# Keys of pairs 13 and 14 loaded whole instead of in parts of three quarters and one quarter

## The chip, the cores and the metric

The kernel runs on one core of one Trainium2 chip. The metric is the device time of one execution in microseconds (us), as a median of several runs.

## The reference

One token of width 512 is normalised; it then goes through attention over a cache of 8192 keys and values for each of 32 heads, and through a small gated block whose result gates the attention's output:

```python
# x [1,1,512], k_cache and v_cache [1,32,8192,128], wq [512,4096], wo [4096,512], all float32
xn = layernorm(x)
q = (xn @ wq) as 32 heads of 128
p = softmax(q . k_cache * 128 ** -0.5)          # per head, over 8192 keys
s = (p . v_cache, heads joined) @ wo
g = silu((sigmoid(xn @ w_gate) * (xn @ w_up)) @ w_down)
out = x + s * g
```

Keys and values are 268 MB; nothing in them is used twice.

## The kernel before

Heads are worked off in 16 pairs (0 to 15). A pair's keys, like its values, fill one buffer: 128 partitions (64 for each head) with 128 positions of 128 numbers each, which is 64 KB a partition and 8 MB in all. There are three such buffers, named slots: keys alternate between two of them (pair i in slot (i+1) % 2), all values go through the third. After the last pair, the output weights wo (8 MB) go into the slot that held pair 14's keys.

All loads of keys, values and wo are issued by SyncE (SP) on one queue, in the order of the code, each behind its waits. `load_keys(i, ...)` waits until pair i-2's scores have been summed, that is until its slot is free; `load_values` waits until PE is done with the values before. From pair 2 on the order is: keys of pair i, then values of pair i-1. Values of pairs 14 and 15 are loaded in halves and smaller parts (`V_CUTS`), the first half as soon as PE has used the first half of the values before.

For each pair, VectorE (DVE) multiplies the keys by the query in place (line 415), sums each product over 128 numbers (line 416), and takes the maximum of the scores (line 418). `K_CUTS` tells for which pairs the keys come in parts; for each part DVE waits for its load, multiplies and sums. Then PE turns the maxima so that DVE can reduce them to one for each head (`all_max`, line 408), ScalarE (ACT) computes the exponentials, which are the weights (`powers_of`, line 430), and PE weighs the values with them in a burst of 64 matmuls (`pair`, tile `slot,zeros`). ACT copies the result out, PE picks the diagonal blocks out of it (tile `o,pick`), and DVE turns them (`heads_out`, line 423).

After pair 15 the heads are divided by the softmax sums and turned into a column (line 472). Then comes the product with wo, loaded in nine pieces (`W_ENDS`): DVE takes 17 of the 32 row blocks (`W_DVE`, lines 513 and 515) and adds its two partial sums (line 518), PE takes 11 others; DVE adds the two results (`to_fold`, line 490), PE folds that into the accumulator that already holds rows 28 to 30 (`fold`), adds the last row, 31, and DVE gates and adds x (lines 537, 539). PE's instructions are all recorded under line 38; its groups are told apart by their tiles.

Of the kernel before, what the change touches and what calls it, by code (L numbers as in the profile page):

```python
# [51 lines left out]
def kernel(  # L52
# [18 lines left out]
    NB = S // HP  # L71
    NP = H // 2
# [18 lines left out]
    W_ENDS, W_FOLD = (10, 16, 20, 23, 26, 28, 30, 31, 32), 28  # L91
    W_PE = [0, 1, 10, 16, 17, 20, 21, *range(24, W_FOLD)]
    W_DVE = [r for r in range(W_FOLD) if r not in W_PE]
    V_CUTS, K_CUTS = (NB // 2, NB * 13 // 16), {NP - 3: (NB * 3 // 4,), NP - 2: (NB * 3 // 4,), NP - 1: (NB // 2,)}

    N_SEMS = 40
    DVE, ACT, SP, POOL = nc.vector, nc.scalar, nc.sync, nc.gpsimd
    PE = Later(nc.tensor)
    pe_only = OrderedEngineSet([nc.tensor.engine])
# [2 lines left out]

    sems = [nc.alloc_semaphore(f"s_{i}") for i in range(N_SEMS)]
    s_out = nc.alloc_semaphore("s_out")
# [494 lines left out]
```

## Time and profile before

| | |
|---|---|
| median of 3 runs | 684.52 us (684.47 to 685.29) |
| the profiled execution | 684.89 us, span 683.4 us |
| busy share of the span: DVE, PE, ACT | 90%, 32%, 7% |
| loads | 293.67 MB, mean 430 GB/s |
| granted TensorE clock, mean | 0.668 of full speed |

Times in the timelines are microseconds from the span's start. A line gives the start, the duration, the engine, the line of the kernel, the operation, output and inputs by the program's names with their shapes, and how many instructions were merged; in brackets the idle time of the engine ahead of it and what ended it. SPq is SyncE's queue; its rows show when loads are issued, not when they land. PEq is PE's sequencer, which waits for semaphores.

### The profile page before, as it was taken

To read this page: it belongs to the slowest core of one execution; us is meant where nothing else is said; L and a number is where in the kernel's file an instruction comes from. 1 tells how busy PE (TensorE), PEld (TensorE's weight loads), DVE (VectorE), ACT (ScalarE), POOL (GpSimd) and SP (SyncE) were. 2 spreads that over 40 slices of the span, in tenths; PEclk is the share of its full clock that TensorE was granted. 3 is DMA by queue.
4 is the path that set the end of the run, shared out by engine and by line. 5 is a ranking of instruction groups with operands and counts; after the bars stand their busy time and mean duration, and the time that the engine had idled before them with its cause. 6 is when DMAs were issued, how large, how long until landed. Compare 5 with 4: busy or idle time off the path is not lost. (4 is left out here: it accounts for less than half of the span.)

```text
span 683.4 us, 3400 instructions
## 1 busy us (share of the span) xinstructions
PE 216.2 (32%) x1376; PEld 62.0 (9%) x1376; DVE 615.2 (90%) x156; ACT 44.6 (7%) x142; POOL 2.6 (0%) x11
## 2 busy tenths in 40 slices
PE   0353024060513206050412406050422406060666
PEld 0120001010100101010100101010100101010110
DVE  3879999999999998998989899898989999999917
ACT  2130010000000101000000100000010101000010
POOL 0000000000000000000000000000000000000000
PEclk9996657575665757575665757575665757575886
DMA  9999999999999999999999999999999999999998
GB/s 382 429 440 472 430 430 430 430 430 430 430 430 430 430 430 430 430 456 456 437 430 430 430 430 430 430 430 430 430 430 445 449 441 399 476 399 430 430 430 337
DMA packets 7552, 293.67 MB, mean 430 GB/s; under 512 B 856, under 2 KB 864, under 8 KB 1664
## 3 DMA queue, kind: packets, MB, share of 16 engines
q1 hardware_dynamic: 7544, 293.67, 99.5%
q10 hardware_dynamic: 8, 0.00, 0.0%
HBM read 293.67 MB, written 0.00 MB: 430 GB/s over the span
## 5 line engine op out<-in xcount | busy, mean ns | idle before, releaser
L415 DVE TENSOR_TENSOR slot<-slot,q_all 128x16384 f32<-128x16384 f32 (+3 forms) x19 | 275.9, 14522 | 21.4 <-DMA slot<-in_A_k_cache_dram 21.4
L416 DVE TENSOR_REDUCE sc<-slot 128x128 f32<-128x16384 f32 (+3 forms) x19 | 276.0, 14525 | 0.7
L38 PE MATMUL psum<-slot,zeros 128*8 128x512 f32 x1024 | 145.5, 727 | 261.5 <-PEq L38 261.5
L38 PEld LDWEIGHTS psum<-slot,zeros 128*8 128x8 f32 x1024 | 30.2, 102 | 363.3 <-issue 363.3
L38 PE MATMUL psum<-ident,mx 128*1 128x128 f32 x32 | 8.7, 372 | 108.6 <-PEq L38 108.6
L437 ACT COPY o<-psum 128x512 f32<-128x512 f32 x16 | 9.4, 586 | 405.1 <-PE psum L38 405.1
L38 PE MATMUL psum<-slot,ones 128*128 (+3 forms) x36 | 15.9, 612 | 21.9 <-PEq L38 16.2
L290 DVE SCALAR_TENSOR_TENSOR slot<-slot,xn 128x1376 f32<-128x1376 f32 (+1 forms) x8 | 18.9, 2360 | 3.0 <-DMA slot<-in_A_wq_dram 2.7
L38 PE MATMUL psum<-o,pick 128*2 128x128 f32 x128 | 16.5, 272 | 12.8 <-PEq L38 12.8
L423 DVE STREAM_TRANSPOSE psum<-psum 32x128 f32<-32x128 f32 x16 | 5.0, 310 | 11.1 <-PE psum L38 11.1
L430 ACT ACTIVATE zeros<-sc,nb 64x128 f32<-64x128 f32 x32 | 12.8, 399 | 0.9
L38 PEld LDWEIGHTS psum<-o,pick 128*2 128x2 f32 x128 | 9.9, 84 | 29.6 <-issue 27.2
L428 ACT ACTIVATE nb<-psum 128x2 f32<-128x2 f32 x16 | 2.8, 172 | 150.9 <-PE psum L38 150.9
L38 PE MATMUL psum<-slot,o_all 128*1 128x128 f32 (+1 forms) x54 | 10.7, 510 | 5.3 <-DMA slot<-in_A_wo_dram 5.3
L38 PEld LDWEIGHTS psum<-ident,mx 128*1 128x1 f32 x32 | 1.9, 80 | 112.6 <-issue 112.6
L408 DVE TENSOR_REDUCE mx<-psum 1x2 f32<-1x128 f32 x16 | 4.4, 277 | 7.8 <-PE psum L38 7.8
L38 PE MATMUL psum<-zeros,rs 128*32 128x2 f32 x32 | 3.8, 188 | 23.5 <-PEq L38 23.5
L38 PE MATMUL psum<-mx,ones 1*128 1x2 f32 x32 | 8.4, 330 | 7.4 <-PEq L38 7.4
L515 DVE SCALAR_TENSOR_TENSOR q_all<-slot,o_all,q_all 128x512 f32<-128x512 f32 x15 | 10.0, 747 | 0.0
L38 PE MATMUL psum<-slot,o 128*1 128x512 f32 x26 | 5.5, 910 | 12.8 <-DMA slot<-in_B_w_down_dram 12.8
L38 PEld LDWEIGHTS psum<-slot,ones 128*128 128x128 f32 (+1 forms) x36 | 6.4, 201 | 31.3 <-issue 23.3
L38 PEld LDWEIGHTS psum<-mx,ones 1*128 1x128 f32 x32 | 7.5, 290 | 14.3 <-issue 14.3
(54 smaller groups left out, 60.5 us busy)
## 6 DMA issues: line engine op xcount, KB each, us to landing
slot<-in_A_k_cache_dram SPq DMA_DIRECT2D x2, 6144.0 KB, 37.9
slot<-in_A_v_cache_dram SPq DMA_DIRECT2D x3, 4096.0 KB, 22.7
slot<-in_A_wq_dram SPq DMA_DIRECT2D x2, 4096.0 KB, 16.3
slot<-in_A_k_cache_dram SPq DMA_DIRECT2D x2, 4096.0 KB, 40.5
slot<-in_A_k_cache_dram SPq DMA_DIRECT2D x2, 2048.0 KB, 42.4
slot<-in_B_w_gate_dram SPq DMA_DIRECT2D x1, 2752.0 KB, 26.7
slot<-in_B_w_up_dram SPq DMA_DIRECT2D x1, 2752.0 KB, 32.7
slot<-in_B_w_down_dram SPq DMA_DIRECT2D x1, 2560.0 KB, 24.1
```

The source lines that it names most:

```text
L38: ins = getattr(self.engine, name)(*args, **kwargs)
L290: return dve(DVE.scalar_tensor_tensor(y, w[:, k, cols], xn[:, k:k + 1], y, op0=ALU.mult, op1=ALU.add))
L408: DVE.reduce_max(mx[:1, 1:3], pt[0:1, :].rearrange("o (e p) -> o e p", e=2), axis=AX.X).then_inc(reduced, 1)
L415: wait(DVE, dve(DVE.tensor_mul(k[:, j, :], k[:, j, :], qb[:, i:i + 1, :].to_broadcast([P, n, Dh]))))
L416: summed[i] = dve(DVE.reduce_sum(sc[i % 2][:, j], k[:, j, :], axis=AX.X))
L423: turned_out[i] = dve(DVE.transpose(o, pn.rearrange("e (a r) -> e a r", r=WR)))
L428: wait(ACT, act(ACT.mul(nb, pm[:, :2], -SCALE)))
L430: ACT.activation(weights[h, :, e * HT:(e + 1) * HT], sc[i % 2][h].rearrange("p (g b) -> p g b", b=HT), AF.Exp, bias=nb[h, e:e + 1], scale= ...
L437: ACT.copy(o1, po).then_inc(copied, 1)
L515: ins = DVE.scalar_tensor_tensor(part[n], wo_t[:, r, :], col, part[n], op0=ALU.mult, op1=ALU.add)
```

## The change

Pairs 13 and 14 are taken out of the table of cuts, so their keys are loaded, multiplied and summed whole, as those of pairs 0 to 12 are. Pair 15 keeps its two halves. Two semaphores are no longer needed.

```diff
-    V_CUTS, K_CUTS = (NB // 2, NB * 13 // 16), {NP - 3: (NB * 3 // 4,), NP - 2: (NB * 3 // 4,), NP - 1: (NB // 2,)}
+    V_CUTS, K_CUTS = (NB // 2, NB * 13 // 16), {NP - 1: (NB // 2,)}
 
-    N_SEMS = 40
+    N_SEMS = 38
```

On DVE, at pair 14 (`slot` the keys, `q_all` the queries, `sc` the scores, `mx` the maxima):

```order
 L408 TENSOR_REDUCE mx<-psum 1x2
-L415 TENSOR_TENSOR slot<-slot,q_all 128x12288
-L416 TENSOR_REDUCE sc<-slot 128x96
-L415 TENSOR_TENSOR slot<-slot,q_all 128x4096
-L416 TENSOR_REDUCE sc<-slot 128x32
+L415 TENSOR_TENSOR slot<-slot,q_all 128x16384
+L416 TENSOR_REDUCE sc<-slot 128x128
 L418 TENSOR_REDUCE mx<-sc 128x1
 L423 STREAM_TRANSPOSE psum<-psum 32x4x32
```

Product and sum of three quarters and of one quarter become one product and one sum over all 128 positions; what stands ahead of them and behind keeps its place. Pair 13 changes in the same way.

On SP's queue, from the values of pair 12 on:

```order
 L227 DMA slot<-in_A_v_cache_dram 128x16384
-L168 DMA slot<-in_A_k_cache_dram 128x12288
-L168 DMA slot<-in_A_k_cache_dram 128x4096
+L168 DMA slot<-in_A_k_cache_dram 128x16384
 L227 DMA slot<-in_A_v_cache_dram 128x16384
 L168 DMA slot<-in_A_k_cache_dram 128x8192 x2
```

The two loads of pair 14's keys become one between the values of pairs 12 and 13; pair 15's keys still follow as two halves.

## The prediction

> **What bounds the kernel now.** I read the slices and the queue table of the page first, then the chain of waits, then the timelines of VectorE (DVE), TensorE (PE) and SyncE's queue (SP) over the last 220 us, last the granted clock. From the page:
>
> ```profile
> DMA  9999999999999999999999999999999999999998
> q1 hardware_dynamic: 7544, 293.67, 99.5%
> ```
>
> The one load queue keeps the 16 DMA engines busy for 99.5% of the span. Less compute cannot shorten that; only a dry queue, or a tail behind the last bytes that gets longer, can move the time. The chain that ended last:
>
> ```profile
> 641.64 5.35 PE psum L38 x32
> ...
> 650.71 28.58 DMA slot<-in_A_wo_dram
> ...
> 679.95 0.62 PE psum L38 x16
> ...
> 680.59 0.44 PE psum L38 x8
> ```
>
> It ends in the loads of wo, whose last pieces release the last products at 679.95 and 680.59. So DVE and PE may be late only by what they wait for wo. DVE's timeline (start, duration; in brackets the idle time before and who ended it):
>
> ```profile
> 467.47 17.23 DVE L415 TENSOR_TENSOR slot<-slot,q_all 128x16384 f32<-128x16384 f32 x1 [2.77 <-DMA slot<-in_A_k_cache_dram]
> ...
> 506.12 17.23 DVE L415 TENSOR_TENSOR slot<-slot,q_all 128x16384 f32<-128x16384 f32 x1 [2.80 <-DMA slot<-in_A_k_cache_dram]
> ...
> 540.64 0.29 DVE L418 TENSOR_REDUCE mx<-sc 128x1 f32<-128x128 f32 x1
> ...
> 541.90 12.94 DVE L415 TENSOR_TENSOR slot<-slot,q_all 128x12288 f32<-128x12288 f32 x1
> ...
> 576.65 0.29 DVE L418 TENSOR_REDUCE mx<-sc 128x1 f32<-128x128 f32 x1
> ...
> 578.62 12.96 DVE L415 TENSOR_TENSOR slot<-slot,q_all 128x12288 f32<-128x12288 f32 x1 [0.84 <-DMA slot<-in_A_k_cache_dram]
> ...
> 613.38 0.29 DVE L418 TENSOR_REDUCE mx<-sc 128x1 f32<-128x128 f32 x1
> ...
> 614.80 8.67 DVE L415 TENSOR_TENSOR slot<-slot,q_all 128x8192 f32<-128x8192 f32 x1
> ...
> 649.55 0.29 DVE L418 TENSOR_REDUCE mx<-sc 128x1 f32<-128x128 f32 x1
> ...
> 664.76 0.32 DVE L423 STREAM_TRANSPOSE psum<-psum 32x128 f32<-32x128 f32 x1 [10.40 <-PE psum L38]
> ...
> 665.34 0.21 DVE L472 STREAM_TRANSPOSE o_all<-psum 32x32 f32<-32x32 f32 x1
> 667.00 0.88 DVE L513 TENSOR_SCALAR q_all<-slot,o_all 128x512 f32<-128x512 f32 x2 [1.46 <-DMA slot<-in_A_wo_dram]
> 667.80 10.02 DVE L515 SCALAR_TENSOR_TENSOR q_all<-slot,o_all,q_all 128x512 f32<-128x512 f32 x15
> 677.86 0.69 DVE L518 TENSOR_TENSOR q_all<-q_all 128x512 f32<-128x512 f32 x1
> 679.15 0.69 DVE L490 TENSOR_TENSOR q_all<-q_all,psum 128x512 f32<-128x512 f32 x1 [0.60 <-PE psum L38]
> ```
>
> Pairs 11 and 12 (whole keys) wait 2.8 us for their keys; pairs 13 to 15 (in parts) hardly wait: DVE is ahead of the loads there. PE's timeline, from pair 3 on:
>
> ```profile
> 216.36 8.31 PE L38 MATMUL psum<-slot,zeros 128*8 128x512 f32 x64 [15.15 <-PEq L38]
> ...
> 525.55 9.02 PE L38 MATMUL psum<-slot,zeros 128*8 128x512 f32 x64 [19.91 <-PEq L38]
> ...
> 544.07 0.24 PE L38 MATMUL psum<-zeros,rs 128*32 128x2 f32 x2 [1.39 <-PEq L38]
> 564.24 8.45 PE L38 MATMUL psum<-slot,zeros 128*8 128x512 f32 x64 [19.93 <-PEq L38]
> ...
> 602.92 9.59 PE L38 MATMUL psum<-slot,zeros 128*8 128x512 f32 x64 [22.81 <-PEq L38]
> ...
> 631.94 5.30 PE L38 MATMUL psum<-slot,zeros 128*8 128x512 f32 x32 [14.99 <-PEq L38]
> ...
> 652.56 0.24 PE L38 MATMUL psum<-zeros,rs 128*32 128x2 f32 x2 [1.39 <-PEq L38]
> 652.71 7.72 PE L38 MATMUL psum<-slot,zeros 128*8 128x512 f32 x52
> 661.03 1.89 PE L38 MATMUL psum<-slot,zeros 128*8 128x512 f32 x12 [0.59 <-PEq L38]
> ...
> 680.17 0.40 PE L38 MATMUL psum<-q_all,ones 128*1 128x128 f32 x8
> ```
>
> A burst of 64 matmuls weighs one pair's values. Pairs 0 to 13 do it in one go, in 8.31 (pair 3, the shortest) to 9.59 us (pair 13, the longest of 14). Pair 15's burst, from 652.71, pauses at 52 for its last 1.5 MB and goes on at 661.03: what bounded it was the load, not PE.
>
> **The change, part by part.** It removes two loads and four instructions of DVE; the same bytes are loaded in the same order, and PE, ACT and POOL keep their instructions.
>
> *The loads.* Values of pairs 11, 12 and 13 arrived (first matmul of the burst) at 525.55, 564.24 and 602.92: 38.69 and 38.68 us apart, with the keys of 13 and 14 in two parts between them. Whole keys of pairs 11 and 12 arrived 38.65 us apart (467.47, 506.12). So a part more costs the queue 0.03 to 0.04 us; two fewer give at most -0.1 us. I count 0.
>
> *Arrival.* Whole keys of pair 13 arrive at 506.12+38.65 = 544.77, those of pair 14 at 583.42. DVE loses its early start: 541.90 becomes 544.77, 578.62 becomes 583.42.
>
> *DVE.* A whole pair takes 540.64-506.12 = 34.52 us to its maximum, one in two parts 576.65-541.90 = 34.75, so each merge gives 0.23 back. Pair 13 ends at 544.77+34.52 = 579.29 (+2.64), still before pair 14's keys; so pair 13's lateness goes no further on DVE. Pair 14 ends at 583.42+34.52 = 617.94 (+4.56). To the next product took 541.90-540.64 = 1.26 us; pair 15 starts at 619.20 instead of 614.80, its keys long there, and after 34.75 us (649.55-614.80) its maximum stands at 653.95: **+4.40 us**.
>
> *SP.* Its queue waits for exactly these ends:
>
> ```profile
> 572.76 0.33 SPq L227 DMA_DIRECT2D slot<-in_A_v_cache_dram  x1
> 576.64 0.81 SPq L168 DMA_DIRECT2D slot<-in_A_k_cache_dram  x2
> 609.14 38.68 SPq L227 DMA_DIRECT2D slot<-in_A_v_cache_dram  x5
> ```
>
> Pair 15's keys are issued at 579.3 instead of 576.64. The queue then holds the values of pair 13 (issued 572.76, landed 602.92): 23.6 us of cover, cost 0; without that cover 2.64 us. Behind it on SP stand pair 14's values, which wait for PE until 609.14 anyway. The issue of wo waits for pair 14's sums (617.94), but in SP's order it comes after pair 15's values at 647. Also 0.
>
> *PE before the tail.* Pair 13's weights are ready some 4 us after 579.29, values at 602.92; pair 14's at about 621.5, values at 631.94. Both covered, by 19 and 10 us.
>
> *Pair 15's values: the step that counts.* From maximum to the first matmul of the burst took 652.71-649.55 = 3.16 us; in pair 12, where PE had been idle longer, 544.07-540.64 = 3.43 to the matmul ahead of it, with 0.15 more 3.58. So the burst starts at 657.1 to 657.5, say 657.3, and its values are there by about 661: now it runs in one go, bounded by PE. How long depends on the clock:
>
> ```profile
> 604.00:608.00 4.00, 4.00 (x21) 0.67 (x17) 4.00 (x2) 0.00 (x0) 0.00 (x0) 0.50 0.91 393
> 608.00:612.00 4.00, 4.00 (x44) 1.00 (x36) 3.97 (x2) 0.00 (x0) 0.00 (x0) 0.99 1.12 483
> ...
> 652.00:656.00 4.00, 3.44 (x22) 0.83 (x26) 1.21 (x5) 0.57 (x3) 0.00 (x0) 0.57 1.05 451
> ```
>
> (PE's count is in the second column, the granted clock third from the end.) Pair 13's burst ran at 0.50 for the first 5 us, pair 15's got full clock only near 656. Of the 8.31 to 9.59 us I take the middle, 8.95: end at 666.25 instead of 661.03+1.89 = 662.92, **+3.33 us** (2.5 to 4.2 with both ends of start and burst).
>
> The Trainium skill, "TensorE: Matmul & The Clock Gate", Part 1, says that the clock is doubled after a busy window of some 3.4 us, and that windows run freely. Taken literally (a burst fills one whole window first, so it runs 3.4 to 6.8 us at half clock), and with pair 13's row as the measure (9.59 us with about 5 at half clock, each of which costs half a microsecond), an estimate is 8.7 to 10.4 us, an end at 666.0 to 667.7 and +0.7 to +2.4 us at the finish, +1.6 in the middle, where the rows give +1.0. The trace bears out the lower part of that alone: the longest of 14 bursts took 9.59, the shortest 8.31.
>
> *The tail's slack.* Behind the burst come a copy, picking matmuls and the transposes up to 665.55, which move with it. Then DVE waited for wo until 667.00: 1.4 us absorbed. Its 17 products (10.9 us) run back to back, so no other piece of wo was late for them. Its sum ended at 678.55, and the next addition waited for PE until 679.15: 0.6 absorbed. (PE's own rows of wo absorb the delay too, since they wait for pieces.) That addition ended at 679.84 and PE's folding began at 680.17: 0.3 absorbed. The last row waited for its piece until 680.59, within the folding's 0.40: 0 to 0.2. Together 2.35 (2.3 to 2.5).
>
> *Sum.* 3.33 - 2.35 = **+1.0 us** (ends 0 and +1.9). The profiled execution took 684.89 us (span 683.4 and 1.5 around it), so 685.9; it lies 0.37 above the median of the runs, 684.52, from which the sum is 685.5. I take the latter, since runs are compared by their median.
>
> **The rivals.** *Hidden altogether:* a short burst (8.31) from 657.1 ends at 665.4, +2.5, which the slack swallows: 684.5 to 684.9. For it: every wait of the tail is on wo. Against: the middle burst is a full microsecond over the slack.
>
> *The late clock (slower):* the mechanism is PE's clock in pair 15's burst. If it starts as unluckily as pair 13's (9.59 us from 657.3), it ends at 666.9, +4.0, at the finish +1.6: 686.1 from the median, 686.5 from the profiled run. It decides from a burst of 9.3 us on (3.7-2.35 = 1.37 us, which is 0.2%). For it: bursts cluster near 8.4, 8.95 and 9.5 from pair to pair, so which comes is chance.
>
> *A dry queue (slower):* if pair 15's keys had been what the engines waited for, the 2.64 us would all show: 687.2. It would need 23.6 us of lateness.
>
> *Fewer transfers pay (faster):* the queue is the bound, so a fixed price of each load would come straight off; from the rows 0.04 us each, at most 684.4, and only if the tail hides too. The Trainium skill, "DMA: Bandwidth & Descriptors", Anatomy of one DMA, gives about 2.0 us fixed for each (measured on another issue path than SP's), which by estimate would be 4 us less, 680.5; the arrivals 38.65 and 38.68 apart contradict that as a price of throughput.
>
> **How the numbers follow.** Something like 0.2% (1.37 us) is what a measurement of this kernel can tell. My forecast (+0.4 to +1.37) gets 0.42, hidden 0.20, the late clock or a tail worse than counted 0.30, the dry queue 0.03, faster 0.05. So faster 0.05, same 0.62, slower 0.33. The range goes from the hidden case (684.4) to the late clock from the profiled run (686.6).
>
> **What would show it.** Right: DVE's product of pair 14 starts near 583.4 after some 4 us of waiting for keys; its maximum of pair 15 stands near 654; the burst of pair 15 is one group of 64 ending at 665.4 to 667; DVE's first product with wo starts without a wait for wo near 668.5; folding waits for DVE, and the chain of waits ends over DVE and PE instead of the loads of wo; the DMA share stays above 99%. Wrong: if the keys of pair 14 come earlier than 582, if the values of pair 15 come later than 657, or if the load queue shows a gap near 579 or 603.

## The result and the profile after

The changed kernel takes 686.49 us (median of 19 runs, 685.18 to 688.49), before 685.0 us (19 runs, 684.47 to 685.43): +1.5 us, a ratio of 1.0022 with a 95% interval of 1.0015 to 1.0028. That is a hair beyond what was called "the same". The runs of the changed kernel also lie three times as far apart as those of before; a part of that is time outside the span, 2.3 and 2.5 us in the two longest runs against 1.5 in most, and the spans themselves lie between 683.7 and 686.0. The profiled execution took 685.76 us, its span 684.2 us; the median span of the 19 runs is 684.9, so this profile shows one of the luckier executions.

The load queue is as full as before, on the page of the changed kernel:

```profile
DMA  9999999999999999999999999999999999999997
q1 hardware_dynamic: 7256, 293.67, 99.3%
```

The same bytes come in 288 packets fewer. What differs is the chain that ended last. It no longer holds a load; it goes through DVE:

```profile
666.88 1.05 PE psum L38 x8
...
669.72 3.37 DVE q_all L515 x6
...
679.69 0.70 DVE q_all L518
...
680.49 0.70 DVE q_all L490
...
681.23 0.66 PE psum L38 x16
```

DVE's timeline of the changed kernel (columns as before) shows where the lateness comes from:

```profile
544.49 17.23 DVE L415 TENSOR_TENSOR slot<-slot,q_all 128x16384 f32<-128x16384 f32 x1 [2.97 <-DMA slot<-in_A_k_cache_dram]
...
583.16 17.23 DVE L415 TENSOR_TENSOR slot<-slot,q_all 128x16384 f32<-128x16384 f32 x1 [2.83 <-DMA slot<-in_A_k_cache_dram]
...
618.94 8.67 DVE L415 TENSOR_TENSOR slot<-slot,q_all 128x8192 f32<-128x8192 f32 x1
...
653.68 0.29 DVE L418 TENSOR_REDUCE mx<-sc 128x1 f32<-128x128 f32 x1
...
668.84 0.88 DVE L513 TENSOR_SCALAR q_all<-slot,o_all 128x512 f32<-128x512 f32 x2
```

Pairs 13 and 14 now wait for their keys as pairs 11 and 12 did. Pair 15's product starts at 618.94 instead of 614.80, its maximum stands at 653.68 instead of 649.55, and the first product with wo starts without a wait for wo. PE's timeline of the same kernel:

```profile
657.25 8.83 PE L38 MATMUL psum<-slot,zeros 128*8 128x512 f32 x64
...
681.23 0.40 PE L38 MATMUL psum<-q_all,ones 128*1 128x128 f32 x8 [0.72 <-DVE q_all L490]
```

Pair 15's burst is one piece now and ends at 666.08, 3.16 us later than before (662.92). The folding waits for DVE.

### The profile page after: what moved, and what is told of

It reads as the page before. It is cut to its first block, busy times and chain, and to the rows that moved or that the text cites. A ratio compares the mean times of both kernels' runs of the same rounds, so it can differ in the third digit from the quotient of the medians.

```text
span 684.2 us, 3394 instructions
## 1 busy us (share of the span) xinstructions
PE 221.2 (32%) x1376; PEld 62.5 (9%) x1376; DVE 615.3 (90%) x152; ACT 44.5 (7%) x142; POOL 2.6 (0%) x11
## 5 line engine op out<-in xcount | busy, mean ns | idle before, releaser
L415 DVE TENSOR_TENSOR slot<-slot,q_all 128x16384 f32<-128x16384 f32 (+1 forms) x17 | 275.6, 16213 | 27.7 <-DMA slot<-in_A_k_cache_dram 27.7
L416 DVE TENSOR_REDUCE sc<-slot 128x128 f32<-128x16384 f32 (+1 forms) x17 | 275.7, 16216 | 0.6
L38 PE MATMUL psum<-slot,zeros 128*8 128x512 f32 x1024 | 150.9, 755 | 256.4 <-PEq L38 256.4
```

Source lines behind the costliest of these rows:

```text
L38: ins = getattr(self.engine, name)(*args, **kwargs)
L415: wait(DVE, dve(DVE.tensor_mul(k[:, j, :], k[:, j, :], qb[:, i:i + 1, :].to_broadcast([P, n, Dh]))))
L416: summed[i] = dve(DVE.reduce_sum(sc[i % 2][:, j], k[:, j, :], axis=AX.X))
```

## The experiments

The theory in one line, as it stood after the two traces. DVE's gating (line 537) in the changed kernel, then in before:

```profile
681.92 0.29 DVE L537 TENSOR_TENSOR g_row<-g_row,psum 128x128 f32<-128x128 f32 x1 [0.74 <-PE psum L38]
```

```profile
681.05 0.29 DVE L537 TENSOR_TENSOR g_row<-g_row,psum 128x128 f32<-128x128 f32 x1 [1.21 <-PE psum L38]
```

From the burst's end to that line the changed kernel takes 681.92-666.08 = 15.84 us; before took 681.05-662.92 = 18.13, with waits for wo in it. So the slack is 2.29 us, and a span should be 683.4 + (burst's end - 662.92 - 2.29), or 683.4 where that bracket is negative. Rivals: the whole loads or their later issue cost the load queue; each merge counts alike; the clock has no part.

In the diffs below `...` marks left-out lines; `N_SEMS` follows the number of loads.

**One pair at a time.** Pair 13 whole, pair 14 in parts, against the changed kernel:

```diff
-    V_CUTS, K_CUTS = (NB // 2, NB * 13 // 16), {NP - 1: (NB // 2,)}
+    V_CUTS, K_CUTS = (NB // 2, NB * 13 // 16), {NP - 2: (NB * 3 // 4,), NP - 1: (NB // 2,)}
```

> Pair 13 whole, pair 14 in its two parts. Theory (only DVE's lateness at pair 15's maximum counts, less the 2.35 us that the tail absorbs): pair 13's maximum stands near 579.0, pair 14's first part is there by 578.6 and its product starts near 580.2 instead of 578.62, so pair 15's maximum comes 1.5 us late (651.1), its burst ends by 664 at the latest, and the tail swallows it: 0 to +0.2 us against before. Rival (whole loads cost the load queue, each merge alike): half of the change's +1.5, so +0.7 us.

Measured: 685.25 us, ratio 1.0002 (0.9993 to 1.0011). DVE's timeline:

```profile
580.67 12.93 DVE L415 TENSOR_TENSOR slot<-slot,q_all 128x12288 f32<-128x12288 f32 x1
...
651.22 0.29 DVE L418 TENSOR_REDUCE mx<-sc 128x1 f32<-128x128 f32 x1
...
667.54 0.88 DVE L513 TENSOR_SCALAR q_all<-slot,o_all 128x512 f32<-128x512 f32 x2 [1.27 <-DMA slot<-in_A_wo_dram]
```

Pair 15's maximum is 1.7 us late, and DVE still waits 1.27 us for wo: swallowed. The other way round, pair 14 whole and pair 13 in parts:

```diff
-    V_CUTS, K_CUTS = (NB // 2, NB * 13 // 16), {NP - 1: (NB // 2,)}
+    V_CUTS, K_CUTS = (NB // 2, NB * 13 // 16), {NP - 3: (NB * 3 // 4,), NP - 1: (NB // 2,)}
```

> Pair 14 whole, pair 13 in its two parts. Theory: pair 14's keys arrive near 583.3 whatever pair 13 did, so everything behind them is as with both pairs whole: pair 15's maximum near 653.8 and +0.9 to +1.6 us against before. Rival (each merge alike): +0.7 us.

Measured: 686.48 us, ratio 1.0019 (1.0010 to 1.0028), the whole of the change. In its timeline DVE, done early with pair 13, just waits longer for pair 14:

```profile
583.31 17.23 DVE L415 TENSOR_TENSOR slot<-slot,q_all 128x16384 f32<-128x16384 f32 x1 [5.66 <-DMA slot<-in_A_k_cache_dram]
```

So pair 14 alone pays, and merges do not count alike.

**The lateness without the loads.** All cuts kept, but DVE sums a constant ahead of pair 15's first product:

```diff
+        if i == NP - 1:
+            for _ in range(2):
+                wait(DVE, dve(DVE.reduce_sum(spare, ones.unsqueeze(1).to_broadcast([P, 16, P]), axis=AX.X)))
         scores(i)
```

> The loads of before, all cuts kept; only two sums over a constant (2048 elements each, some 2.2 us each) stand on DVE ahead of pair 15's first product. Theory: pair 15's maximum comes some 4.5 us late (654.1) by another cause than the keys' loads, and the time is that of the change, +0.9 to +1.8 us. Rival (the loads of pairs 13 and 14 themselves cost time): 0 us.

Measured: 686.3 us, ratio 1.0018 (1.0009 to 1.0027). DVE's timeline:

```profile
614.64 4.58 DVE L453 TENSOR_REDUCE spare<-ones 128x16 f32<-128x2048 f32 x2
...
654.03 0.29 DVE L418 TENSOR_REDUCE mx<-sc 128x1 f32<-128x128 f32 x1
```

With every load as before, 4.58 us of idle work cost as much as the change, within the intervals of about half a microsecond. So the lateness alone is enough, and the whole loads need have no part in it. Half of it (one sum):

> The loads of before; one constant sum (2.3 us) on DVE ahead of pair 15's first product. Theory: pair 15's maximum comes 2.3 us late (651.9), its burst starts near 655.3 and ends at 663.6 to 665.4, which the slack of 2.29 us takes almost whole: 0 to +0.3 us, against +1.2 for a stall of twice the length. Rival (every microsecond of lateness counts alike): half of +1.2, +0.6 us.

Measured: 685.01 us, ratio 1.0002 (0.9993 to 1.0011). Pair 15's maximum comes 1.9 us late. Its burst was one of the longest seen, and it still cost nothing (DVE's, then PE's timeline):

```profile
651.44 0.29 DVE L418 TENSOR_REDUCE mx<-sc 128x1 f32<-128x128 f32 x1
```

```profile
654.60 9.82 PE L38 MATMUL psum<-slot,zeros 128*8 128x512 f32 x64
```

It ends at 664.42, 1.50 us behind before's. The lateness is absorbed up to a point, then it shows.

**Past that point.** Pair 15's keys whole as well:

```diff
-    V_CUTS, K_CUTS = (NB // 2, NB * 13 // 16), {NP - 1: (NB // 2,)}
+    V_CUTS, K_CUTS = (NB // 2, NB * 13 // 16), {}
```

> Pair 15's keys whole too. Theory: they arrive near 621.9 and DVE's maximum stands near 656.4, 2.7 us behind the changed kernel's 653.7; the slack is used up, so all of it shows: +2.5 to +3.0 us against the changed kernel, +4.0 to +4.6 against before. Rival (each merge costs the queue or DVE alike, 0.7 us): +2.2 against before.

Measured: 689.5 us, +4.4 against before, ratio 1.0065 (1.0053 to 1.0077). DVE's and then PE's timeline:

```profile
656.67 0.29 DVE L418 TENSOR_REDUCE mx<-sc 128x1 f32<-128x128 f32 x1
```

```profile
660.25 8.66 PE L38 MATMUL psum<-slot,zeros 128*8 128x512 f32 x64
```

Another 3.0 us at the maximum (656.67 against 653.68) are another 3.0 us in the median (689.5 against 686.49): no slack is left.

**The tail.** The changed kernel without two of DVE's row blocks of wo:

```diff
-    W_DVE = [r for r in range(W_FOLD) if r not in W_PE]
+    W_DVE = [r for r in range(W_FOLD) if r not in W_PE and r not in (18, 19)]
```

> The changed kernel with two of DVE's 17 row blocks of wo left out of the product (rows 18 and 19; their part of the result is missing), all loads kept. Theory: DVE's tail is 1.34 us shorter, so of the change's +1.5 us +0.1 to +0.4 is left, and the chain that ends last goes over the loads of wo again in a run with a short burst. Rival (PE's part of the tail or the loads bound the end): +1.2 to +1.5 us as with the change.

Measured: 685.28 us, ratio 1.0005 (0.9996 to 1.0014): 1.2 of the 1.5 us are gone. The profiled run had a long burst (9.26 us, to 667.17), so its chain still went over DVE; two products less (13 instead of 15 in the second group) brought its span to 684.0:

```profile
670.74 8.70 DVE L515 SCALAR_TENSOR_TENSOR q_all<-slot,o_all,q_all 128x512 f32<-128x512 f32 x13
```

**The clock of the burst.** Three attempts to keep PE busy ahead of pair 15's burst with small matmuls (`keep(n)`: n times `PE.matmul(wide[0][0:1, 2 * GC:3 * GC], ones[:, 0:1], ident)`) in the changed kernel. First, 40 ahead of the wait for the maximum, 3 and 10 between the small matmuls behind it:

```diff
+        keep(40)
         taken(maxed, 1)
...
+        keep(3)
         taken(reduced, 1)
...
+        keep(10)
         taken(powers, 2)
```

> The changed kernel, with 53 small matmuls more in each pair on PE (40 ahead of the wait for the maximum, 3 and 10 between the small matmuls behind it), which write to an unused part of a bank; their only effect is to keep PE busy ahead of the burst. Theory: pair 15's burst then runs at full clock from its start and takes 7.2 to 7.8 us instead of 8.83, its end is 2.1 us later than before, less than the 2.35 us of slack: 0 to +0.3 us against before, and runs as close together as those of before. Rival (the burst's clock has no part in it): burst of 8.4 us or more, +1.5 us, runs as far apart as with the change.

Measured: 689.83 us, ratio 1.0071 (1.0058 to 1.0085): missed. PE's timeline says why:

```profile
650.29 8.90 PE L38 MATMUL psum<-ident,ones 128*1 128x128 f32 x80
...
662.54 7.03 PE L38 MATMUL psum<-slot,zeros 128*8 128x512 f32 x61
```

Each took 0.22 us (8.90 us for 40, which the row counts as 80), more than I had allowed, so they ran 5 us past the maximum's due time and everything shifted. But the burst behind them took 7.1 us, shorter than any other before or since the change. With 16, 2 and 5:

> As the kernel with 53 small matmuls more in each pair, but with 23 (16, 2 and 5), at the 0.22 us each that they turned out to take, so that they end before pair 15's maximum (654) instead of 5 us behind it. Theory: the burst starts near 657.3, runs warm, in 7.2 to 7.8 us, and ends by 665.1, 2.2 us later than before, within the slack (2.29 us by the traces so far): 0 to +0.3 us against before instead of +1.5, and the runs no further apart than those of before. Rival (the clock has no part in it): +1.5 us.

Measured: 686.45 us, ratio 1.0024 (1.0015 to 1.0032): missed again.

```profile
647.69 3.66 PE L38 MATMUL psum<-ident,ones 128*1 128x128 f32 x32
655.03 0.58 PE L38 MATMUL psum<-ident,mx 128*1 128x128 f32 x2 [3.69 <-PEq L38]
```

In the profiled run they were over at 651.35, PE idled 3.69 us, and the burst started slow. The third time the fill-in was tied to DVE's progress:

```diff
-    V_CUTS, K_CUTS = (NB // 2, NB * 13 // 16), {NP - 1: (NB // 2,)}
+    V_CUTS, K_CUTS = (NB // 2, NB * 13 // 16), {NP - 1: (NB // 2, NB * 3 // 4)}
...
+    near = semaphore("s_near")
...
+        keep(6)
+        taken(near, 1)
+        keep(14)
         taken(maxed, 1)
...
             wait(DVE, dve(DVE.tensor_mul(k[:, j, :], k[:, j, :], qb[:, i:i + 1, :].to_broadcast([P, n, Dh]))))
+            if j.stop == NB:
+                DVE.nop().then_inc(near, 1)
```

> The changed kernel with 27 small matmuls more in each pair on PE, timed so that they reach up to pair 15's maximum wherever the burst before ended: 6 behind the picking, 14 released by DVE ahead of its last sum, 2 and 5 between the small matmuls behind the maximum. For that, pair 15's second half is computed in two quarters (0.23 us later). Theory: the burst starts near 657.6 at full clock, takes 7.1 to 7.6 us and ends by 665.2, 2.3 us later than before: 0 to +0.3 us against before. Rival (the clock has no part in the time): +1.5 to +1.8 us.

Measured: 688.03 us, ratio 1.0054 (1.0040 to 1.0068). The burst did what the theory says (PE's timeline), and DVE waited for wo again:

```profile
658.51 7.05 PE L38 MATMUL psum<-slot,zeros 128*8 128x512 f32 x64
```

```profile
668.84 0.88 DVE L525 TENSOR_SCALAR q_all<-slot,o_all 128x512 f32<-128x512 f32 x2 [0.63 <-DMA slot<-in_A_wo_dram]
```

The chain that ended last also runs over the loads of wo again:

```profile
by line: DMA slot<-in_A_wo_dram 4.3%; PE psum L38 1.0%; SPq L168 0.4%; SPq L228 0.1%; issue 0.1%; DVE g_row L549 0.0%; DVE g_row L551 0.0%
```

That does not show that a warm burst puts compute back behind the loads of before, since here the loads themselves were late: the first values arrive at 101.6 instead of 100.2, the last row of wo is released at 682.44 instead of 680.59:

```profile
682.44 0.44 PE psum L38 x8
```

Nor could the second attempt have shown it: there the last piece but one of wo released PE at 681.33, in before at 679.95, so by estimate the loads alone would have held its span at 683.4+1.4 = 684.8 us. Where the lateness comes from is not settled. All three kernels with the added matmuls have the late first values, and their queue tables hold a row that before and the changed kernel lack; from the last of them:

```profile
q8 instruction: 1, 0.02, 0.0%
```

So the time of a kernel with nothing but a warm burst was not obtained. With the burst's end at 665.56 (658.51+7.05) and the loads of before, the formula would give 683.75, an estimate that no run has tested.

**More samples of the clock.** The changed kernel itself three times more:

> The changed kernel again, for another sample of the clock. Theory: the span is 683.4 + (end of pair 15's burst - 662.92) - 2.29; the burst starts near 657.3 and lasts 8.3 to 10.4 us as the clock happens to rise, so the span goes with it one to one from 683.7 to 685.8. Rival: spans differ by something else (arrival of the loads), and the burst's length does not go with them.

> As the run before it: the same formula has to give this span from this burst's end within 0.3 us.

> As the two runs before it. By the median of the runs (+1.5 us) the burst's median over all runs should be near 9.4 us rather than the 8.95 of the prediction.

Measured: 686.79, 685.84 and 686.53 us, one run each. The bursts in their PE timelines:

```profile
657.78 9.32 PE L38 MATMUL psum<-slot,zeros 128*8 128x512 f32 x64
```

```profile
657.59 8.39 PE L38 MATMUL psum<-slot,zeros 128*8 128x512 f32 x64
```

```profile
656.89 9.95 PE L38 MATMUL psum<-slot,zeros 128*8 128x512 f32 x64
```

The granted clock (last column but two) in the shortest of these:

```profile
657.00:660.00 3.00, 2.57 (x14) 0.50 1.03 438
660.00:661.00 1.00, 1.00 (x12) 0.83 1.11 475
```

and in the longest:

```profile
660.00:662.00 2.00, 2.00 (x16) 0.50 0.95 410
662.00:663.00 1.00, 1.00 (x12) 0.61 1.14 492
```

Full clock came 2.7 us after the burst's start in one (0.83 is two thirds of that slice at full clock, so from 660.34), 5.9 us after it in the other (from 662.78). The same view of pair 13's bursts, in the first of these two runs and in the second:

```profile
605.00:606.00 1.00, 1.00 (x9) 0.64 1.06 459
```

```profile
608.00:609.00 1.00, 1.00 (x12) 0.92 0.45 197
```

There full clock came at 605.72 and at 608.16. Read the same way in all four profiles of the changed kernel:

| profile | pair 13's burst | full clock | pair 15's burst | full clock | between the two rises |
|---|---|---|---|---|---|
| changed kernel | 602.57 | 606.26 | 657.25 | 660.88 | 54.62 |
| again, first | 603.11 | 607.78 | 657.78 | 662.40 | 54.62 |
| again, second | 602.90 | 605.72 | 657.59 | 660.34 | 54.62 |
| again, third | 602.43 | 608.16 | 656.89 | 662.78 | 54.62 |

The two rises lie the same time apart wherever the bursts start. In before they lie 655.86-608.08 = 47.78 us apart. In the trace of the changed kernel the rises of pairs 0, 1 and 2 (104.50, 142.06 and 183.02) are 37.56 and 40.96 us apart. All four distances fit whole steps of 3.413 us: 16 (54.61), 14 (47.78), 11 (37.54) and 12 (40.96). So within one execution the clock rises on a grid, whose place differs from one execution to the next.

The median of the four bursts is 9.08 us, not the 9.4 expected; the median of their four spans is 684.65, below the 684.9 of the 19 runs. The formula against the profiled spans:

| run | burst ends | formula | span |
|---|---|---|---|
| changed kernel | 666.08 | 684.3 | 684.2 |
| again, first | 667.10 | 685.3 | 685.3 |
| again, second | 665.98 | 684.2 | 684.1 |
| again, third | 666.84 | 685.0 | 685.0 |
| pair 14 alone whole | 665.93 | 684.1 | 684.1 |
| two sums ahead of pair 15 | 667.10 | 685.3 | 685.3 |
| one sum ahead of pair 15 | 664.42 | 683.4 | 683.3 |
| two row blocks left out (less 10.02-8.70 = 1.32) | 667.17 | 684.0 | 684.0 |
| pair 15 whole too | 668.91 | 687.1 | 687.5 |
| 40, 3 and 10 matmuls | 669.57 | 687.8 | 687.8 |
| 16, 2 and 5 matmuls | 666.99 | 685.2 | 685.2 |

The first row fixed the slack, so it tests nothing; the other ten do. Only one is off by more than 0.1: with pair 15 whole, PE's folding and last row took 1.07 instead of 0.66 us, at a granted clock of 0.51 instead of 1.00, after 3.70 us of waiting for DVE. Not in the table are pair 13 alone whole (formula 683.4, span 684.0), where the loads of wo came half a microsecond later and, as in before, set the end, and the third kernel with added matmuls, whose loads were late.

## Why the prediction was right, and which size was off

The mechanism held at every step: DVE's lateness, less what the tail absorbs, reached the end. The size was low. Forecast were +1.0 us and 685.5; measured are +1.49 (interval +1.0 to +1.9) and 686.49. Half of the missing microsecond is the base: 684.52 was the median of three runs, that of 19 is 685.0. That 686.49 still lies in the range, 0.1 us below its top, is partly luck: the top was set from the profiled execution of before, 0.37 us above that base. Of the cases, the likeliest (+0.4 to +1.37, chance 0.42) was just missed, and the median falls to the next, the late clock or a tail worse than counted (0.30). The threshold of that case has a small slip: 3.7-2.35 is 1.35, not 1.37.

- **No gain or loss at the queue:** right. The DMA share stayed above 99%, and before's loads with a late DVE cost the same as the change.
- **Arrival and DVE:** right. Keys of pair 14 at 583.16 (forecast 583.42), maximum of pair 15 at 653.68 (653.95), lateness 4.13 us (4.40). The wait ahead of pair 14's product is 2.83 us, not some 4: the 4.16 from the maximum of pair 13 to that product hold DVE's own small steps too.
- **Pair 13 harmless:** right, by pair 13 alone (1.0002) against pair 14 alone (1.0019); with pair 14 whole, pair 15's maximum stands at 653.68 with pair 13 whole and at 653.83 with it in parts.
- **SP's cover and PE before the tail:** right. Pair 15's keys were never waited for, and the values of pairs 13 and 14 set their bursts.
- **Burst start:** right, 656.9 to 657.8 over four profiles of the changed kernel (657.3).
- **Burst length:** the term that was mis-sized. 8.95 us was the middle of the earlier bursts; four profiles of the changed kernel show 8.83, 9.32, 8.39 and 9.95. By the formula the median span of 684.9 means an end at 666.7 and, from the mean start of 657.4, a burst of some 9.3 us; that is inferred, and the four that were measured average 9.1. By the inferred length the burst carries 0.38 us of the half microsecond between +1.0 and +1.5; a start 0.08 us later and a slack 0.06 us smaller make up the rest. The rival of the late clock was the same mechanism with a larger number, and 9.3 us is the very length from which it was said to decide.
- **Which comes is chance:** only from one execution to the next. Within one, the grid of 3.41 us fixes it: bursts 38.65 us apart (11.3 steps) meet little more than three places in a step, so the 14 bursts of one trace fell in three clusters, whose middle was taken. Over the bursts of 64 of all profiles, apart from those with PE kept busy just ahead of them, full clock came 2.6 to 6.0 us after the start and the burst took 8.31 to 10.00 us. The middle of that, 9.15, would have made the forecast +1.2, by estimate.
- **The page's rule:** the estimate from the Trainium skill, "TensorE: Matmul & The Clock Gate", Part 1, that I weighed as too pessimistic gave 8.7 to 10.4 us and +1.6 in the middle. The trace agrees with windows that run freely, by the table of rises above. It does not agree with a whole window ahead of full clock: that came as early as 2.75 us after the start of a burst of pair 15, and the four bursts took 8.39 to 9.95 us. That +1.6 came nearer to +1.5 than +1.0 did is partly luck: its middle, 9.55 us, lies above the inferred 9.3 and the measured mean of 9.1.
- **Slack:** 2.35 forecast, 2.29 measured. The waits were counted some 0.1 us too long each, since DVE needs that between dependent steps without a wait too (668.73 to 668.84 in the changed kernel); the share of the last row was near its upper end.
- **No faster from fewer transfers:** right; pair 13's merge alone, one transfer fewer, gives 1.0002 (0.9993 to 1.0011), which leaves no room for 2 us a transfer.

That the load queue stays full while the time grows is the point of the case: the change moved the end from the loads of wo to compute, and only what lies beyond the slack shows.

## What to carry to other kernels

In a kernel bound by its load queue, price a delay on another engine by following it to the end and subtracting every wait that lies on the way. Here 1.9 us of lateness at DVE's last maximum cost nothing, 4.1 cost 1.5 and 7.1 cost 4.4. Splitting a load near the end paid here at pairs 14 and 15, which set DVE's last maximum, and not at pair 13, whose lateness ended in the wait for pair 14's keys. When a burst of matmuls comes on the end's path, it brings its clock's chance with it: expect the runs to spread, and take its length from all phases of the clock, not from the few that one trace holds.

## What the runs showed of the hardware that was not expected

- The same 64 matmuls, in the same place of the same program, took 8.39 to 9.95 us from one execution to the next, as full clock came 2.7 to 5.9 us after their start; with small matmuls until just before them, 7.05 us. Within one execution the rises lay whole steps of 3.41 us apart.
- An idle time of 3.69 us ahead of the small matmuls was enough for the clock to fall back to half before the burst. Less was enough in before: with small matmuls between idle times of 1.20, 0.46 and 1.39 us the clock stood at 0.72 in the slice 652 to 653 and at 0.50 in the next.
- Some dozens of small matmuls more in PE's loop went with a load of 0.02 MB on a queue named instruction and with first values 1.3 us later than in the changed kernel (101.57, 101.54 and 101.61 against 100.27). That one causes the other was not tried.
